# Attention with a fused GEGLU feed-forward on one core: cutting the work that is interleaved between attention passes into smaller pieces, reordering it, and moving loads

## The chip, the cores and the metric

The kernel runs on one core of a Trainium2 chip. The metric is the device time of one execution in microseconds (us). Times of engines, waits and transfers come from one profiled execution of each kernel.

## The reference

A pre-LayerNorm transformer layer in bf16: 2048 tokens, width 576, 32 heads of 18, feed-forward width 4608.

```python
def _A_ref(x, wqkv, wo):                      # attention, H = 32, Dh = 18
    ...
    scores = jnp.einsum("bhqd,bhkd->bhqk", q, k) * (Dh ** -0.5)
    p = _softmax(scores, axis=-1)
    o = jnp.einsum("bhqk,bhkd->bhqd", p, v)
    return (...)(o, 0, 2, 1, 3).reshape(B, S, D) @ wo

def _B_ref(x, w_gate, w_up, w_down):          # GEGLU, tanh gelu
    return (_gelu(x @ w_gate) * (x @ w_up)) @ w_down

h  = x + _A_ref(_layernorm(x), A_wqkv, A_wo)
h2 = h + _B_ref(_layernorm(h), B_w_gate, B_w_up, B_w_down)
```

## The kernel before

The tokens are cut into four blocks of 512 queries, each block into eight units of four heads, each unit into 32 passes. A *pass* is two score matmuls, one exponential and half a group of probability-times-value (PV) matmuls. Score tiles live in `Sring`, which has two slots, so PE can be at most two passes ahead of ACT:

```python
def emit_ST(i):                    # PE: two score matmuls of pass i
    ...
    slot = i % 2
    ...
    pe_group(fns, reads=[("KTj", s_), ("QTj", s_)], writes=wkeys)

def emit_EXP(i):                   # ACT: one exponential of 128x1024
    E("act", lambda e: e.activation(PT[:, pts, :], Sring[:, slot * 1024:(slot + 1) * 1024], ACTF.Exp, scale=SCALE),
      reads=[("S", slot * 2), ("S", slot * 2 + 1)], writes=[("PT", pts)])
```

Between passes the emitter puts *fillers*: pieces of the feed-forward (FFN) of the block before. A filler has a ready time in passes and a cost; each pass brings 560 of credit, and a filler is emitted whole:

```python
def run_fillers(i, budget):
    while urgent and urgent[0][0] <= i:
        _, _, fn = urgent.pop(0)
        fn()
    credit[0] = min(credit[0] + budget, 3 * budget)
    while bulk and bulk[0][0] <= i and credit[0] > 0:
        ready, cost, fn, tag = bulk.pop(0)
        fn()
        credit[0] -= cost
```

The FFN of one block has two halves of 18 gate/up steps and five down tiles each:

```python
def ffn_gate_up(f, slot, tail=False):         # PE: 5 + 5 matmuls, two evacuations
    ...
def ffn_gelu_a(f, tail=False):                # x*x (POOL; in the tail ACT), product (DVE), add (DVE; in the tail POOL)
def ffn_gelu_b(f):                            # tanh (ACT)
def ffn_gelu_c(f):                            # product (DVE), times up (POOL), into gT
def ffn_down(hf, m, slot):                    # PE: 18 matmuls, one evacuation
    ...
at(s0, 2200.0, ... ffn_gate_up(f, slot, tail=tl))
at(s0 + 2, 0.0, ... ffn_gelu_a(f, tail=tl))
at(s0 + 6, 0.0, ... ffn_gelu_b(f))
at(s0 + 8, 0.0, ... ffn_gelu_c(f))
...
at(s0 - 3, 0.0, ... ffn_load_wd(wslot, hf, m, barrier=(b == 0)))
at(s0, GS * 220.0, ... ffn_down(hf, m, wslot))
```

At a block's end come the output projection (Wo), LayerNorm 2 and its transposes, for four tiles of 128 rows. All loads go through one in-order queue, issued by SP; `jit_loads(u + 1)` fetches K, Q and V of the next unit eight passes ahead, as four K and four Q transfers of 19 partitions each:

```python
for c in range(4):
    j, r0 = head_loc(4 * g + c)
    pairs.append((KTj[32 * c:32 * c + PS, s_, :], KTd[r0:r0 + PS, j, :]))
...
    pairs.append((QTjm[32 * c:32 * c + PS, s_, c, :], QTd[r0:r0 + PS, j, b * QB:(b + 1) * QB]))
```

After the last block its own FFN is left over with no attention to lie between: the *tail*.

## Time and profile before

| stretch of the kernel before | from to (us) | what sets the pace |
|---|---|---|
| prologue and attention of block 0 | 0 to 426 | not touched by the change |
| three blocks with FFN fillers | 426 to 1512 | PE and ACT by turns |
| tail: Wo, LayerNorm 2 and the last FFN | 1512 to 1764 | one chain through DVE, POOL and ACT |

The median was 1767.25 us of four runs. These are the page's busy times (engine, busy us, share, instructions), its granted PE clock in 40 slices (tenths of full speed) and two of its costliest groups (busy, mean ns of one, then the idle time just before them and what ended it):

```profile
PE 1402.6 (80%) x7386; PEld 512.7 (29%) x7528; DVE 739.6 (42%) x1572; ACT 1109.5 (63%) x1293; POOL 370.4 (21%) x364
PEclk9778999999899999998999999989999999588988
L578 ACT ACTIVATE PT<-Sring 128x1024 bf16<-128x1024 f32 x1024 | 960.8, 1048 | 351.1 <-PE Sring L296 346.3
L296 PE MATMUL Sring<-QTjm,KTj 128*128 128x512 bf16 x1933 | 591.0, 388 | 133.3 <-ACT PT L578 105.0 <-issue 14.3 <-DMA QTjm<-QTd 9.3
```

Read the last two rows together. ACT stood idle 346 us in front of exponentials until PE had scores; PE stood idle 105 us in front of scores until ACT had emptied a slot. Two engines that wait for each other are the sign of pieces that are too coarse for the buffer between them.

### The profile page before, as it was taken

How to read it: one execution, taken by the hardware profiler on the slowest of the kernel's cores; microseconds unless marked ns; L12 is line 12 of the kernel's file. 1: busy time of each engine (PE TensorE's matmuls, PEld its weight loads, DVE VectorE, ACT ScalarE, POOL GpSimd, SP SyncE). 2: the span in 40 equal slices, each digit the busy share in tenths (PEclk: the TensorE clock that was granted, in tenths of full speed). 3: DMA queues.
4: the chain of work that ended last, by engine and by line, in shares of the span. 5: the costliest groups of instructions: out<-in, count | busy, mean ns of one | idle time of the engine just before them, and what ended most of it. 6: DMA issues, size and time to landing. Idle time of an engine off the chain costs nothing.

```text
span 1763.7 us, 20592 instructions
## 1 busy us (share of the span) xinstructions
PE 1402.6 (80%) x7386; PEld 512.7 (29%) x7528; DVE 739.6 (42%) x1572; ACT 1109.5 (63%) x1293; POOL 370.4 (21%) x364
## 2 busy tenths in 40 slices
PE   1558998887788899887898998878988988475765
PEld 0223332112232333233332332333323333321322
DVE  7546651002355046314551363144622651454352
ACT  2123789998577678676785786767866866133230
POOL 1000000000044034200340243003421430044251
PEclk9778999999899999998999999989999999588988
DMA  3010000000123212211232122111231221122332
GB/s 101 14 39 7 10 10 17 11 17 11 37 68 80 60 42 66 64 45 31 63 88 61 35 63 63 46 47 50 63 76 43 62 64 34 41 63 71 87 81 47
DMA packets 193173, 87.22 MB, mean 49 GB/s; under 512 B 97968, under 2 KB 190064, under 8 KB 193072
## 3 DMA queue, kind: packets, MB, share of 16 engines
q1 hardware_dynamic: 193072, 85.91, 18.2%
q8 instruction: 59, 0.97, 0.2%
q14 instruction: 42, 0.34, 0.1%
HBM read 71.07 MB, written 2.36 MB: 42 GB/s over the span
## 4 chain that ended last, share of the span: by engine, by line
PE 42%; ACT 20%; issue 19%; POOL 9%; DVE 8%; DMA 1%; SPq 1%; POOLq 0%; ACTq 0%; DVEq 0%
PE G L296 24%; ACT PT L578 19%; PE Sring L296 13%; POOL arena L721 3%; PE Aacc L297 3%; POOL arena L703 2%; POOL arena L700 2%; PE G L309 1%; SPq L288 1%; DVE arena L701 1%; POOL lnt L395 1%; DMA arena<-in_B_w_up_dram 1%; DVE kmx L437 1%; DVE kmx L439 1%; ACT arena L710 1%
## 5 line engine op out<-in xcount | busy, mean ns | idle before, releaser
L578 ACT ACTIVATE PT<-Sring 128x1024 bf16<-128x1024 f32 x1024 | 960.8, 1048 | 351.1 <-PE Sring L296 346.3
L296 PE MATMUL Sring<-QTjm,KTj 128*128 128x512 bf16 x1933 | 591.0, 388 | 133.3 <-ACT PT L578 105.0
L296 PE MATMUL G<-hnT,arena 128*128 128x512 bf16 x1421 | 356.0, 399 | 55.9 <-ACT arena L317 45.9
L296 PE MATMUL G<-arena 128*128 128x512 bf16 (+4 forms) x1112 | 267.4, 397 | 53.9 <-issue 40.9
L296 PEld LDWEIGHTS Sring<-QTjm,KTj 128*128 128x128 bf16 x2048 | 136.2, 98 | 434.1 <-ACT PT L578 331.5
L721 POOL TENSOR_TENSOR arena<-arena 128x512 bf16<-128x512 bf16 x144 | 166.2, 1154 | 392.9 <-DVE arena L719 384.9
L296 PEld LDWEIGHTS G<-hnT,arena 128*128 128x128 bf16 x1440 | 140.5, 101 | 248.9 <-ACT arena L317 64.6
L297 PE MATMUL Aacc<-PT,Vpj 128*32 128x512 bf16 x2048 | 205.9, 392 | 0.7 <-ACT PT L578 0.7
L719 DVE SCALAR_TENSOR_TENSOR arena<-arena 128x512 bf16<-128x512 bf16 x144 | 99.7, 692 | 178.7 <-ACT arena L710 178.7
L296 PEld LDWEIGHTS G<-arena 128*128 128x128 bf16 (+3 forms) x1120 | 118.3, 113 | 190.7 <-issue 91.3
L710 ACT ACTIVATE arena<-arena 128x512 bf16<-128x512 bf16 x144 | 91.6, 636 | 121.6 <-POOL arena L703 94.8
L701 DVE SCALAR_TENSOR_TENSOR arena<-arena 128x512 bf16<-128x512 bf16 x144 | 118.8, 825 | 104.7 <-POOL arena L700 104.1
L700 POOL TENSOR_TENSOR arena<-arena 128x512 bf16<-128x512 bf16 x108 | 112.4, 1041 | 199.0 <-DVE arena L322 199.0
L297 PEld LDWEIGHTS Aacc<-PT,Vpj 128*32 128x32 bf16 x2048 | 52.6, 93 | 221.6 <-issue 217.9
L324 DVE TENSOR_SCALAR arena<-G 128x512 bf16<-128x512 f32 x144 | 98.2, 682 | 13.4 <-PE G L296 13.4
L395 POOL TENSOR_TENSOR lnt<-lnt,halfc 128x1 f32<-128x1 f32 x32 | 17.6, 550 | 402.7 <-DVE lnt L394 342.2
L554 POOL COPY Vpj<-Vd 128x1152 bf16<-128x1152 bf16 x32 | 36.7, 1148 | 309.5 <-PE Aacc L297 296.0
L322 DVE CAST arena<-G 128x512 bf16<-128x512 f32 x108 | 73.8, 684 | 37.4 <-PE G L296 37.3
L598 DVE CAST a_sb<-Aacc 128x512 bf16<-128x512 f32 x32 | 22.1, 691 | 150.4 <-PE Aacc L297 150.2
L735 DVE COPY arena<-G 128x512 f32<-128x512 f32 (+1 forms) x20 | 13.8, 690 | 137.5 <-PE G L296 137.5
L317 ACT ACTIVATE arena<-G 128x512 bf16<-128x512 f32 x36 | 20.9, 580 | 65.4 <-PE G L296 65.4
L703 POOL TENSOR_TENSOR arena<-arena 128x512 bf16<-128x512 bf16 x36 | 41.4, 1150 | 56.7 <-DVE arena L701 56.7
(79 smaller groups left out, 556.3 us busy)
## 6 DMA issues: line engine op xcount, KB each, us to landing
arena<-in_B_w_gate_dram SPq DMA_DIRECT2D x72, 256.0 KB, 2.7
arena<-in_B_w_up_dram SPq DMA_DIRECT2D x72, 256.0 KB, 3.2
arena<-in_B_w_down_dram SPq DMA_DIRECT2D x32, 576.0 KB, 5.0
KTj<-KTd SPq DMA_DIRECT2D x128, 76.0 KB
QTjm<-QTd SPq DMA_DIRECT2D x128, 19.0 KB
arena<-in_A_x_dram SPq DMA_DIRECT2D x4, 576.0 KB, 3.9
h_sb<-in_A_x_dram SPq DMA_DIRECT2D x4, 576.0 KB, 5.9
arena<-in_B_w_gate_dram SPq DMA_DIRECT2D x72, 32.0 KB, 2.7
```

Of the source, the lines that this page charges most:

```text
L296: return lambda e: e.matmul(dst, lhsT, rhs, start=start, stop=stop)
L297: return lambda e: e.matmul(dst, lhsT, rhs, start=start, stop=stop, tile_position=tile_position, skip_group_check=skip)
L322: E("dve", lambda e: e.tensor_copy(dst_ap, src_ap), reads=reads, writes=writes)
L324: E("dve", lambda e: e.tensor_scalar(dst_ap, src_ap, scale, None, ALU.mult), reads=reads, writes=writes)
L554: E("pool", lambda e: e.tensor_copy(dst, src), reads=[("Vd", kt) for kt in range(NKT)] + [("Vd", kt, 1) for kt in range(NKT)], writes=[("V ...
L578: E("act", lambda e: e.activation(PT[:, pts, :], Sring[:, slot * 1024:(slot + 1) * 1024], ACTF.Exp, scale=SCALE), reads=[("S", slot * 2), ...
L700: E("pool", lambda e: e.tensor_tensor(x2, xb, xb, ALU.mult), reads=[("xb", k)], writes=[("x2", k)])
L701: E("dve", lambda e: e.scalar_tensor_tensor(out=x2, in0=x2, scalar=GC1, in1=xb, op0=ALU.mult, op1=ALU.mult), reads=[("x2", k), ("xb", k)], ...
L703: E("pool" if tail else "dve", lambda e: e.tensor_tensor(x2, x2, xb, ALU.add), reads=[("x2", k), ("xb", k)], writes=[("x2", k)])
L710: E("act", lambda e: e.activation(th, uu, ACTF.Tanh, scale=GC0), reads=[("x2", k)], writes=[("th", k)])
L719: E("dve", lambda e: e.scalar_tensor_tensor(out=x2, in0=th, scalar=1.0, in1=xb, op0=ALU.add, op1=ALU.mult), reads=[("th", k), ("xb", k)], ...
L721: E("pool", lambda e: e.tensor_tensor(gT[:, fs, :], x2, ub, ALU.mult), reads=[("ub", k), ("x2", k)], writes=[("gT", fs)])
```

## The change

Its intent is to make the fillers small enough for the two score slots, and to keep their inputs ready. Gate and up become two fillers of five matmuls; a down becomes three of six; Wo becomes 10 + 15, with all four Wo before the four LayerNorm-2 transposes; the second half of a gelu is emitted after the first half of the next one; down weights are prefetched, two tiles at a half's start; the next unit's K/Q/V load goes 24 instead of 8 passes ahead; the K projection of a tile is queued as five items instead of one.

```diff
-    def ffn_gate_up(f, slot, tail=False):
+    def ffn_gate(f, slot, tail=False):
         ...
+    def ffn_up(f, slot):
         ...
+    DCH = 3
-    def ffn_down(hf, m, slot):
+    def ffn_down_part(hf, m, slot, part):
+        ...
+        lo, hi = part * per, min(GS, (part + 1) * per)
+        ...
+        pe_group(fns, reads=[("wd", slot)] + [("gT", fs) for fs in range(lo, hi)], writes=[bkey])
 ... schedule_ffn ...
+                if fs == 0:
+                    for m in range(min(2, NIT)):
+                        at(s0, 0.0, ... ffn_load_wd(ws, hf, m, barrier=(b == 0)))
-                at(s0, 2200.0, ... ffn_gate_up(f, slot, tail=tl))
-                at(s0 + 2, 0.0, ... ffn_gelu_a(f, tail=tl))
-                at(s0 + 6, 0.0, ... ffn_gelu_b(f))
-                at(s0 + 8, 0.0, ... ffn_gelu_c(f))
+                at(s0, 1100.0, ... ffn_gate(f, slot, tail=tl))
+                at(s0 + 1, 1100.0, ... ffn_up(f, slot))
+                at(s0 + 3, 0.0, ... ffn_gelu_a(f, tail=tl))
+                if fs > 0:
+                    at(s0 + 5, 0.0, ... ffn_gelu_b(f - 1))
+                    at(s0 + 7, 0.0, ... ffn_gelu_c(f - 1))
 ...
-                at(s0 - 3, 0.0, ... ffn_load_wd(wslot, hf, m, barrier=(b == 0)))
-                at(s0, GS * 220.0, ... ffn_down(hf, m, wslot))
+                for part in range(DCH):
+                    at(s0 + part, 1320.0, ... ffn_down_part(hf, m, ws, part))
+                at(s0 + DCH - 1, 0.0, ... ffn_down_evac(hf, m))
+                if m + 2 < NIT:
+                    at(s0 + DCH - 1, 0.0, ... ffn_load_wd(ws, hf, m2))
 ... schedule_block_end ...
-            add_bulk(base + 7 + 2 * qt, 1800.0, ... block_Wo_qt(b, qt))
-            add_bulk(base + 9 + 2 * qt, 0.0, ... block_LN2_stats(b, qt))
-            add_bulk(base + 14 + 2 * qt, 600.0, ... block_LN2_T(b, qt))
+            add_bulk(base + 7 + 2 * qt, 900.0, ... block_Wo_qt_a(b, qt))
+            add_bulk(base + 8 + 2 * qt, 1100.0, ... block_Wo_qt_b(b, qt))
+            add_bulk(base + 8 + 2 * qt, 0.0, ... block_LN2_stats(b, qt))
+        for qt in range(4):
+            add_bulk(base + 17 + qt, 600.0, ... block_LN2_T(b, qt))
 ... main loop ...
-            if p == NPASS_U - 8:
+            if p == NPASS_U - 24:
                 if u + 1 < NU:
                     jit_loads(u + 1)
```

## The prediction

> **What bounds the kernel now.** Times are microseconds (us). One *pass* is two 128x512 score matmuls on PE, one 128x1024 exponential on ACT, and half a group of four PV matmuls; the program has 1024 of them, 256 for each block of 512 queries. Between passes the emitter puts *fillers*: the FFN of the block before. I first cut the span into stages (busy time of each engine by window; columns: stretch, length, busy time of PE, PEld, DVE, ACT, POOL with instruction counts, granted PE clock, DMA share, GB/s):
>
> ```profile
> 0.00:445.00 445.00, 321.13 (x1736) 113.46 (x1769) 186.33 (x436) 287.86 (x336) 22.77 (x40) 0.93 0.07 23
> 445.00:1506.00 1061.00, 918.05 (x4954) 329.44 (x5051) 435.71 (x928) 758.62 (x849) 262.56 (x248) 0.97 0.21 56
> 1506.00:1764.00 258.00, 163.43 (x697) 69.83 (x708) 117.53 (x209) 63.03 (x108) 85.09 (x76) 0.80 0.27 67
> ```
>
> Prologue and block 0 take 445, three blocks with FFN fillers 1061 (354 each), and a tail without attention 258. In the middle stretch PE is busy 87% and ACT 72%: neither is full, so one is being made to wait for the other. The timeline of PE shows how. First one period of gate/up filler (start, duration, idle before it):
>
> ```profile
> 656.06 2.32 PE L296 MATMUL G<-hnT,arena 128*128 128x512 bf16 x10
> 658.22 0.59 PE L296 MATMUL Sring<-QTjm,KTj 128*128 128x512 bf16 x2
> 658.75 0.40 PE L297 MATMUL Aacc<-PT,Vpj 128*32 128x512 bf16 x4
> 659.08 0.61 PE L296 MATMUL Sring<-QTjm,KTj 128*128 128x512 bf16 x2
> 659.93 0.60 PE L296 MATMUL Sring<-QTjm,KTj 128*128 128x512 bf16 x2 [0.25 <-ACT PT L578]
> ...
> 661.29 2.32 PE L296 MATMUL G<-hnT,arena 128*128 128x512 bf16 x10
> ```
>
> Ten filler matmuls hold PE for 2.16 (656.06 to 658.22); ACT, with room for two score tiles only, runs dry. Then four passes follow in which PE waits for ACT. Period 5.23. The down filler is longer, and the first down of each half also waits (the record says "issue") for the last gelu:
>
> ```profile
> 572.10 5.73 PE L296 MATMUL G<-arena 128*128 128x512 bf16 x18 [3.41 <-issue]
> 583.49 4.05 PE L296 MATMUL G<-arena 128*128 128x512 bf16 x18
> 593.62 4.06 PE L296 MATMUL G<-arena 128*128 128x512 bf16 x18
> ```
>
> One period is 10.13 with seven passes in it. At a block's end PE stands before the LayerNorm-2 transposes, which come right after the next Wo:
>
> ```profile
> 457.56 0.85 PE L309 MATMUL G<-ident,hn 128*128 128x128 bf16 x5 [4.25 <-DVE hn L404]
> ```
>
> The tail is another regime. One gate/up step there, DVE, POOL and ACT:
>
> ```profile
> 1563.63 0.69 DVE L719 SCALAR_TENSOR_TENSOR arena<-arena 128x512 bf16<-128x512 bf16 x1 [1.93 <-ACT arena L710]
> ...
> 1564.40 1.15 POOL L721 TENSOR_TENSOR arena<-arena 128x512 bf16<-128x512 bf16 x1 [1.47 <-DVE arena L719]
> 1564.84 1.26 DVE L701 SCALAR_TENSOR_TENSOR arena<-arena 128x512 bf16<-128x512 bf16 x1
> ...
> 1566.18 1.15 POOL L703 TENSOR_TENSOR arena<-arena 128x512 bf16<-128x512 bf16 x1 [0.63 <-DVE arena L701]
> ...
> 1567.36 0.63 ACT L710 ACTIVATE arena<-arena 128x512 bf16<-128x512 bf16 x1 [2.62 <-POOL arena L703]
> ...
> 1568.02 0.69 DVE L719 SCALAR_TENSOR_TENSOR arena<-arena 128x512 bf16<-128x512 bf16 x1 [1.92 <-ACT arena L710]
> ```
>
> This is one serial chain: second product (DVE), times up (POOL), first product of the next step (DVE), add (POOL), tanh (ACT), period 4.39, no engine full.
>
> **What the Trainium skill says.** "TensorE: Matmul & The Clock Gate", Part 1 (the HAM clock gate): a 512-column matmul starts every 215.7 ns warm and 426.7 ns cold, and PE goes cold after an idle window of about 3.4 us. The trace agrees: 2.16 / 10 = 216 ns here, and after the 3.41 wait above the 18 matmuls took 5.73 instead of 4.06. The same page, Part 3 (packing small matmuls): 32-column matmuls in different column groups run concurrently. So do the four PV matmuls: 0.33 for four (658.75 to 659.08). "SBUF — State Buffer", "Who interferes with whom": a DVE instruction with two SBUF inputs and a POOL instruction that reads SBUF exclude each other, for the whole instruction. The trace agrees: the first product takes 0.68 alone, but 1.26 when it starts inside L721, and ends at 1566.10, 0.55 after L721 (1565.55).
>
> **The change, part by part.** No instruction is added or removed on PE but the order changes; I read the order as built.
>
> (a) Gate and up (five matmuls each) become two fillers, and the built order is, over long stretches: four score matmuls, four PV, five filler matmuls. PE's need for four passes and one step: per two passes 0.43 + 0.53 + 0.33 = 1.29 (start-to-start above), per five fillers 1.08; together 2.37, for four passes 4.74. ACT's need: four exponentials at 0.94 (3.77 for four in the timeline) plus a tanh of 0.65 = 4.4. ACT can lag at most two tiles; laying the two out by hand (a score pair to its exponential's start 0.64, exponential 1.02, release 0.06) I find every score matmul's tile free at least about 0.0 to 0.7 before it is wanted, so PE should run without waiting. I take 4.78: saved 0.45 x 36 steps x 3 blocks = 49.
>
> (b) Down splits into 6 + 6 + 6. PE needs 7 x 0.645 + 3.88 = 8.4 against 10.13; ACT needs 6.6. Saved 1.73 x 10 x 3 = 52.
>
> (c) A part of down waits for its own six gT tiles only, and two more parts lie between it and the last gelu. The wait of 3.41 to 4.13 at six first downs, and about 1.5 of cold clock after each, go. I count 4.5 x 6 = 27.
>
> (d) All four Wo go before the four LN2 transposes; the DVE chain of one tile is 4.4 long and is now hidden under Wo and passes. Per block 4.25 + 1.3 (a smaller wait of the same kind) + about 1 cold = 6.5; x 3 = 20.
>
> (e) The gelu's second half of step f-1 goes behind the first half of step f. In the overlapped blocks this only adds latency that nobody waits for. In the tail it takes the tanh off the chain, but the two DVE products and the two POOL products still exclude each other: 0.6 + 0.69 + 1.15 + 1.15 = 3.59. So 4.39 becomes about 3.6, not the 2.3 that POOL alone would need: 0.8 x 36 = 29.
>
> (f) Tail, the rest: Wo and LN2 31 (7.6 each) becomes DVE-bound, about 2.6 + 4 x 4.4 + 3 = 23: 8. Down parts that start before the last gelu (idle there 9.05 and 8.80): about 3 each, 6.
>
> (g) Loads. Down weights are prefetched two at a half's start, in the one in-order queue before the second gate/up chunk. In the first FFN the two are chained by waits for landings: I estimate 6 lost. The next unit's K/Q load goes 24 instead of 8 passes ahead; no wait on it stood on the path (0.66 at 864), so nothing is gained, but its issue takes 11 in front of gate/up chunks; the three waits of about 1.1 for a chunk (503, 864, 1229) may come to some 3 each as steps get shorter: 6 more. Splitting the K tile filler changes nothing: the four parts have the same ready number, all urgent items that are ready are emitted at once, and the built PE order is identical up to the first Wo. So the first 445 stay.
>
> Sum: 49 + 52 + 27 + 20 - 12 = 136 in the blocks, 29 + 8 + 6 = 43 in the tail, 179 together: 1767 - 179 = 1588. Check from above: a block's PE need is 256 x 0.645 + 540 FFN matmuls x 0.216 + some 12 for Wo and transposes = 294, and some 40 passes without filler go at ACT's 0.92 instead of 0.645, 11 more: 305, against 354 - 136/3 = 309. The two agree.
>
> **The rivals.** First: ACT takes PE's place as what ends last. For it: ACT is within 7% of PE in the gate/up stretch (4.4 against 4.74), and a tanh that waits for DVE blocks the exponentials behind it. Against: a tanh is now emitted a whole step after its input is. If true, the step falls to 5.0 only and half of (a) is lost: about 1615. Second: DVE or the shared port. DVE needs 3.2 a step and the locked instructions about 4.0 (0.69 x 2 + 0.42 + 1.04 + 1.15) of 4.74; if evacuations get late, PE waits for a G bank. With three banks an evacuation has about two fillers' time (4.7) of slack. If it happened, steps stay near 5.2: about 1640. Third: in the tail the port lock doesn't bind (the skill's rule, one case in the trace): then the step falls to about 2.5 and the time to 1550. Fourth: the prefetched weights crowd the queue and each half's start stalls: + 3 to 5 at each of eight halves, about 1620. That all gain vanishes would need the filler gaps to come back elsewhere; with PE at 87% and ACT at 72% I see nothing that would hold it.
>
> **Range and chances.** Predicted 1588. Rivals one, two and four pull up, three down, so the range is lopsided: 1562 to 1630. 2% is 35 us; losing four fifths of the sum is needed to stay within it. Faster 0.97, same 0.02, slower 0.01.
>
> **What would show it.** In the profile after: gate/up periods of 4.7 to 4.9 with PE busy over 95% there and no wait for ACT between passes; downs at 8.4 to 8.7 per three parts; no wait of 3 to 4 before the first down nor before an hn transpose; tail steps of 3.5 to 3.7 with the two DVE products stretched; the time up to the first Wo unchanged. Gate/up at 5.2 with PE waiting for DVE, or ACT at 95%, would prove (a) wrong; tail steps at 4.4 or 2.5 prove (e) wrong.

## The result, and the profile after

The changed kernel takes 1596.74 us (median of 8 runs, 1596.11 to 1598.73), beside 1767.69 for the kernel before (13 runs, 1764.82 to 1770.59). The ratio is 0.9035, 95% interval 0.9026 to 0.9043: faster. A ratio is the mean time of one kernel's runs over that of the other's of the same rounds, so not quite the ratio of the medians. The result is 9 us above the 1588 predicted, inside the range.

The same lines of the page as before, and the same three windows of busy time by engine (the middle one is now 947 long instead of 1061, the tail 205 instead of 258):

```profile
PE 1345.6 (84%) x7386; PEld 509.7 (32%) x7528; DVE 761.7 (48%) x1572; ACT 1114.2 (70%) x1293; POOL 397.7 (25%) x364
PEclk9778999999988999999999999999999999979898
L578 ACT ACTIVATE PT<-Sring 128x1024 bf16<-128x1024 f32 x1024 | 976.7, 1040 | 255.9 <-PE Sring L296 254.0
L296 PE MATMUL Sring<-QTjm,KTj 128*128 128x512 bf16 x1963 | 567.5, 385 | 75.5 <-ACT PT L578 58.2
```

```profile
0.00:445.00 445.00, 324.14 (x1781) 115.47 (x1815) 189.37 (x450) 291.49 (x340) 23.42 (x42) 0.93 0.07 23
445.00:1392.00 947.00, 873.52 (x4909) 332.10 (x5005) 441.41 (x913) 759.00 (x846) 262.91 (x247) 0.98 0.25 64
1392.00:1597.00 205.00, 147.90 (x697) 62.10 (x708) 130.94 (x209) 63.75 (x109) 111.41 (x76) 0.89 0.32 80
```

Both mutual waits shrank: 346 to 254 and 105 to 58. In the middle stretch PE was idle for 1061 - 918 = 143 before and for 947 - 874 = 74 now. ACT's work there did not change (758.62 and 759.00).

For the reading by parts I cut both timelines of PE at the first matmul of each stage. Sums over the three blocks, and in brackets the exponentials in the stage (a pass on the edge counts twice):

| stage, three blocks | before | after | difference |
|---|---|---|---|
| first Wo to first gate | 119.2 (75) | 85.2 (69) | -34.0 |
| gate/up, both halves, with the wait before the first down | 604.4 (431) | 544.8 (419) | -59.6 |
| down of half 0 | 158.3 (108) | 140.3 (111) | -18.0 |
| down of half 1, to the next block's Wo | 203.7 (146) | 200.7 (167) | -3.0 |
| **blocks** | **1085.4** | **970.9** | **-114.5** |
| tail: Wo and LayerNorm 2 | 31.5 | 22.1 | -9.4 |
| tail: gate/up, two halves | 166.7 | 106.7 | -60.0 |
| tail: downs and end | 53.9 | 69.7 | +15.8 |
| **tail** | **252.1** | **198.5** | **-53.6** |

The first Wo came at 427.24 instead of 426.22: +1.0. Together -114.5 - 53.6 + 1.0 = -167.1, the difference of the two profiled spans. The last stage of a block seems to gain nothing, but over the three blocks it now holds 21 passes more: a block has a fixed 256 passes, and those that shorter fillers no longer cover are run at the end without fillers, some 0.92 each.

The timeline of PE in the gate/up stage after:

```profile
504.65 1.25 PE L296 MATMUL G<-hnT,arena 128*128 128x512 bf16 x5
505.74 1.03 PE L296 MATMUL Sring<-QTjm,KTj 128*128 128x512 bf16 x4
506.70 0.40 PE L297 MATMUL Aacc<-PT,Vpj 128*32 128x512 bf16 x4
507.03 1.25 PE L296 MATMUL G<-hnT,arena 128*128 128x512 bf16 x5
508.12 1.03 PE L296 MATMUL Sring<-QTjm,KTj 128*128 128x512 bf16 x4
509.08 0.40 PE L297 MATMUL Aacc<-PT,Vpj 128*32 128x512 bf16 x4
```

From 504.65 to 507.03 is 2.38: half a step with two passes, PE without a gap. The whole step is 4.76 instead of 5.23. The downs, by contrast, still have a wait in each period (only their own lines and the waits are shown):

```profile
563.05 1.46 PE L296 MATMUL G<-arena 128*128 128x512 bf16 x6
...
566.95 0.61 PE L296 MATMUL Sring<-QTjm,KTj 128*128 128x512 bf16 x2 [1.14 <-ACT PT L578]
...
573.00 1.47 PE L296 MATMUL G<-arena 128*128 128x512 bf16 x6
...
576.02 0.60 PE L296 MATMUL Sring<-QTjm,KTj 128*128 128x512 bf16 x2 [0.35 <-ACT PT L578]
```

The first down (563.05) starts with no wait before it, where the kernel before stood 3.41. The larger waits of PE in the first block's end and first FFN:

```profile
443.09 0.57 PE L309 MATMUL G<-ident,hn 128*128 128x128 bf16 x5 [1.42 <-DVE h_sb L654]
447.25 0.57 PE L309 MATMUL G<-ident,hn 128*128 128x128 bf16 x5 [1.79 <-DVE hnT L322]
459.72 2.31 PE L296 MATMUL G<-hnT,arena 128*128 128x512 bf16 x5 [5.60 <-DMA arena<-in_B_w_up_dram]
490.66 1.91 PE L296 MATMUL G<-hnT,arena 128*128 128x512 bf16 x4 [9.62 <-DMA arena<-in_B_w_up_dram]
```

The transposes (L309) no longer stand 4.25, but the first FFN waits 15.2 for its weights, where the longest such wait before was 3.61. The second of these loads stood directly behind a K/Q load in the queue (the queue's timeline):

```profile
469.37 2.50 SPq L288 DMA_DIRECT2D KTj<-KTd  x4
471.91 8.76 SPq L288 DMA_DIRECT2D QTjm<-QTd  x4
480.71 1.96 SPq L288 DMA_DIRECT2D arena<-in_B_w_gate_dram  x2
```

And one step of the tail:

```profile
1460.45 1.60 POOL L746 TENSOR_TENSOR arena<-arena 128x512 bf16<-128x512 bf16 x1
...
1461.19 1.41 DVE L744 SCALAR_TENSOR_TENSOR arena<-arena 128x512 bf16<-128x512 bf16 x1
...
1462.02 1.59 POOL L728 TENSOR_TENSOR arena<-arena 128x512 bf16<-128x512 bf16 x1
...
1463.13 1.03 DVE L726 SCALAR_TENSOR_TENSOR arena<-arena 128x512 bf16<-128x512 bf16 x1
...
1463.58 1.60 POOL L746 TENSOR_TENSOR arena<-arena 128x512 bf16<-128x512 bf16 x1
```

The step is 1463.58 - 1460.45 = 3.13 (4.39 before). POOL runs without a gap, but its operations are 1.60 long instead of 1.15.

### The profile page after: what moved, and what is told of

Same layout as the page of the kernel before. It is cut to its first block, busy times and chain, and to the rows that moved or that the text cites. A ratio compares the mean times of both kernels' runs of the same rounds, so it can differ in the third digit from the quotient of the medians.

```text
span 1596.6 us, 20508 instructions
## 1 busy us (share of the span) xinstructions
PE 1345.6 (84%) x7386; PEld 509.7 (32%) x7528; DVE 761.7 (48%) x1572; ACT 1114.2 (70%) x1293; POOL 397.7 (25%) x364
## 4 chain that ended last, share of the span: by engine, by line
PE 41%; issue 16%; ACT 13%; POOL 10%; DVE 9%; SPq 7%; DMA 4%; POOLq 0%; ACTq 0%; DVEq 0%
PE G L296 22%; PE Sring L296 15%; ACT PT L578 12%; SPq L288 7%; POOL arena L746 5%; PE Aacc L297 4%; DMA arena<-in_B_w_up_dram 3%; POOL arena L725 3%; POOL arena L728 1%; PE G L309 1%; POOL lnt L395 1%; DVE kmx L437 1%; DVE kmx L439 1%; DVE h_sb L654 1%; DVE stats L388 1%
## 5 line engine op out<-in xcount | busy, mean ns | idle before, releaser
L578 ACT ACTIVATE PT<-Sring 128x1024 bf16<-128x1024 f32 x1024 | 976.7, 1040 | 255.9 <-PE Sring L296 254.0
L296 PE MATMUL Sring<-QTjm,KTj 128*128 128x512 bf16 x1963 | 567.5, 385 | 75.5 <-ACT PT L578 58.2
L296 PE MATMUL G<-hnT,arena 128*128 128x512 bf16 x1402 | 360.1, 389 | 51.5 <-DMA arena<-in_B_w_up_dram 33.6
L296 PEld LDWEIGHTS Sring<-QTjm,KTj 128*128 128x128 bf16 x2048 | 161.7, 98 | 342.0 <-ACT PT L578 175.5
L746 POOL TENSOR_TENSOR arena<-arena 128x512 bf16<-128x512 bf16 x144 | 180.0, 1250 | 282.0 <-DVE arena L744 282.0
L296 PEld LDWEIGHTS G<-hnT,arena 128*128 128x128 bf16 x1440 | 125.4, 99 | 234.3 <-issue 53.2
L296 PEld LDWEIGHTS G<-arena 128*128 128x128 bf16 (+3 forms) x1120 | 113.6, 112 | 156.8 <-issue 48.1
L744 DVE SCALAR_TENSOR_TENSOR arena<-arena 128x512 bf16<-128x512 bf16 x144 | 128.4, 891 | 65.8 <-ACT arena L735 60.6
L725 POOL TENSOR_TENSOR arena<-arena 128x512 bf16<-128x512 bf16 x108 | 112.5, 1041 | 109.6 <-DVE arena L322 98.3
L726 DVE SCALAR_TENSOR_TENSOR arena<-arena 128x512 bf16<-128x512 bf16 x144 | 109.2, 758 | 46.4 <-POOL arena L725 46.0
L297 PEld LDWEIGHTS Aacc<-PT,Vpj 128*32 128x32 bf16 x2048 | 52.5, 92 | 219.7 <-issue 213.3
L598 DVE CAST a_sb<-Aacc 128x512 bf16<-128x512 f32 x32 | 22.1, 689 | 178.2 <-PE Aacc L297 178.2
L728 POOL TENSOR_TENSOR arena<-arena 128x512 bf16<-128x512 bf16 x36 | 56.4, 1565 | 39.3 <-DVE arena L726 39.3
```

The lines of the kernel that those rows point to most:

```text
L296: return lambda e: e.matmul(dst, lhsT, rhs, start=start, stop=stop)
L297: return lambda e: e.matmul(dst, lhsT, rhs, start=start, stop=stop, tile_position=tile_position, skip_group_check=skip)
L725: E("pool", lambda e: e.tensor_tensor(x2, xb, xb, ALU.mult), reads=[("xb", k)], writes=[("x2", k)])
L726: E("dve", lambda e: e.scalar_tensor_tensor(out=x2, in0=x2, scalar=GC1, in1=xb, op0=ALU.mult, op1=ALU.mult), reads=[("x2", k), ("xb", k)], ...
L728: E("pool" if tail else "dve", lambda e: e.tensor_tensor(x2, x2, xb, ALU.add), reads=[("x2", k), ("xb", k)], writes=[("x2", k)])
L744: E("dve", lambda e: e.scalar_tensor_tensor(out=x2, in0=th, scalar=1.0, in1=xb, op0=ALU.add, op1=ALU.mult), reads=[("th", k), ("xb", k)], ...
```

## The experiments

All twelve kernels gave correct results; runs of the kernel before: medians 1766.6 to 1770.3. "Against the changed kernel" is the difference of the medians to 1596.7. My theory was the prediction's list of parts; the rivals are in the expectations. e1 to e5 and e12 undo one part each, e6 to e9 alter one term, e11 puts one part alone into the kernel before, e10 combines.

| run | edit | median | ratio to before (95%) | against the changed kernel |
|---|---|---|---|---|
| e1_gu_joined | gate and up as one filler | 1650.2 | 0.9327 (0.9312, 0.9342) | +53 |
| e2_down_joined | down as one filler of 18 | 1674.4 | 0.9471 (0.9451, 0.9490) | +78 |
| e3_gelu_old | tanh and product not deferred | 1637.9 | 0.9254 (0.9234, 0.9274) | +41 |
| e4_wo_old | block end as before | 1638.0 | 0.9260 (0.9245, 0.9275) | +41 |
| e5_jit8 | K/Q/V load 8 passes ahead | 1677.0 | 0.9479 (0.9464, 0.9494) | +80 |
| e12_wd_late | down weights not prefetched | 1652.2 | 0.9346 (0.9323, 0.9368) | +55 |
| e11_before_jit24 | kernel before, K/Q/V load 24 ahead | 1817.1 | 1.0287 (1.0261, 1.0313) | (+49 on before) |
| e6_first_early | first FFN's weights loaded earlier | 1580.1 | 0.8930 (0.8913, 0.8946) | -17 |
| e7_jit_split | K/Q/V load in three parts | 1592.4 | 0.9001 (0.8985, 0.9017) | -4 |
| e8_tail_mult_dve | tail: one POOL product to DVE | 1596.9 | 0.9028 (0.9013, 0.9042) | 0 |
| e9_down5 | downs in parts of 5, 5, 5, 3 | 1578.1 | 0.8928 (0.8904, 0.8952) | -19 |
| e10_best | combination | 1521.3 | 0.8608 (0.8585, 0.8631) | -75 |

The seventh part of the change, the K tile filler, was not run: with the old filler put back, the built program has the same instructions in the same order on every engine.

### e1_gu_joined: gate and up in one filler again

```diff
-                at(s0, 1100.0, ... ffn_gate(f, slot, tail=tl))
-                at(s0 + 1, 1100.0, ... ffn_up(f, slot))
+                at(s0, 2200.0, ... (ffn_gate(f, slot, tail=tl), ffn_up(f, slot)))
```

> The changed kernel, but gate and up emitted together again as one filler of ten matmuls; the gelu order, down parts, Wo and loads stay changed. Theory (filler length: ACT runs dry behind ten matmuls): the period of a gate/up step in the blocks goes from 4.76 back to about 5.2, 108 steps x 0.45 = 49 us more, less some 8 us of weight-chunk waits that longer steps hide: 1632 to 1646 us; the tail stays at 198. Rival (the gelu's new place is what smooths the step): time stays within 5 us of 1597 and the step at 4.8.

Measured 1650.2, +53, a little over the range expected. The waits for ACT are back between passes (timeline of PE, one period):

```profile
652.82 2.33 PE L296 MATMUL G<-hnT,arena 128*128 128x512 bf16 x10
...
656.70 0.60 PE L296 MATMUL Sring<-QTjm,KTj 128*128 128x512 bf16 x2 [0.36 <-ACT PT L578]
657.62 0.60 PE L296 MATMUL Sring<-QTjm,KTj 128*128 128x512 bf16 x2 [0.31 <-ACT PT L578]
```

The gate/up stages took 97.1 to 98.4 where the changed kernel takes 87.5 to 88.9; the first, which also waits for its loads, took 108.9 instead of 103.3. The two-slot buffer is the reason that a filler's length matters: ten matmuls hold PE for 2.16, longer than the two exponentials (2 x 0.94) it can have stored.

### e2_down_joined: a down in one piece again

```diff
-    DCH = 3
+    DCH = 1
-                    at(s0 + part, 1320.0, ...
+                    at(s0 + part, GS * 220.0, ...
```

> The changed kernel, but each down is one filler of eighteen matmuls again (its weight prefetch stays as changed). Theory: down periods in the blocks go from 9.2 back to 10.3 to 11 us (1.3 x 30 = 39) and the first down of a half waits 3 to 4 us for the last gelu and runs cold (6 x 3 = 18 net of the 1.1 that is left now), and the tail's first downs start later, 2 x 3: 1640 to 1660 us. Rival (seven passes of ACT work hide behind a long filler anyway): under 1610 us.

Measured 1674.4, +78: more than I had expected. The down stage of half 0 went back to 53.5 (46.9 in the changed kernel), and the gate/up stages to 93 to 95 (the first to 108.9), because the wait before the first down is back inside them (569.26: 5.80 long, and the 18 matmuls after it took 6.61 instead of 4.06, cold, that is at the lower clock that PE is granted after such a wait). Splitting the down gave (b) and (c) of the prediction; as measured below they are worth some 32 and 27, 59 together. Most of the other 19 can be read from the trace: the waits before the six first downs are longer than in the kernel before, 5.58 to 6.19 each and 34.9 in all instead of 22.6, and the tail takes 5 more. PE's waits for weights are not the reason: 34.6 here, 35.2 in the changed kernel. So the parts are not independent. The deferred gelu, which this run keeps, may be what makes those waits longer; that was not run.

### e3_gelu_old: tanh and second product of a step not deferred

```diff
-                if fs > 0:
-                    at(s0 + 5, 0.0, ... ffn_gelu_b(f - 1))
-                    at(s0 + 7, 0.0, ... ffn_gelu_c(f - 1))
-                if fs == GS - 1:
-                    ...
+                at(s0 + 7, 0.0, ... ffn_gelu_b(f))
+                at(s0 + 9, 0.0, ... ffn_gelu_c(f))
```

> The changed kernel, but tanh and both products of a step again right behind its own first half. Theory: it matters in the tail alone: steps there go from 3.12 back to 4.39 us, 36 x 1.27 = 46, less about 6 because the first downs no longer wait for two steps' gelu at the end: 1632 to 1645 us, block stages unchanged within 2 us each. Rival: in the blocks the tanh blocks the exponentials behind it (DVE is behind), so block stages grow by 5 us or more each as well: over 1650 us.

Measured 1637.9, +41, in the theory's range. The tail's two gate/up stages took 74.8 and 73.7 instead of 52.5 and 54.2. The three blocks together took 970.1, in the changed kernel 970.9 (one by one within 4.1 us; single stages differ by up to 6.7, more than the 2 expected, because passes moved between them). One tail step, by its add on POOL and the tanh after it:

```profile
1482.07 1.15 POOL L728 TENSOR_TENSOR arena<-arena 128x512 bf16<-128x512 bf16 x1 [0.63 <-DVE arena L726]
1483.25 0.63 ACT L735 ACTIVATE arena<-arena 128x512 bf16<-128x512 bf16 x1 [2.62 <-POOL arena L728]
...
1486.46 1.15 POOL L728 TENSOR_TENSOR arena<-arena 128x512 bf16<-128x512 bf16 x1 [0.63 <-DVE arena L726]
```

1486.46 - 1482.07 = 4.39: exactly the chain of the kernel before, with its waits. So within the changed kernel the deferral gives the whole gain of the tail's steps and nothing in the blocks.

### e4_wo_old: the block end as before

```diff
-            add_bulk(base + 7 + 2 * qt, 900.0, ... block_Wo_qt_a(b, qt))
-            add_bulk(base + 8 + 2 * qt, 1100.0, ... block_Wo_qt_b(b, qt))
 ...
+            add_bulk(base + 7 + 2 * qt, 1800.0, ... (block_Wo_qt_a(b, qt), block_Wo_qt_b(b, qt)))
+            add_bulk(base + 9 + 2 * qt, 0.0, ... block_LN2_stats(b, qt))
+            add_bulk(base + 14 + 2 * qt, 600.0, ... block_LN2_T(b, qt))
```

> The changed kernel, but Wo in one filler per tile and each LayerNorm-2 transpose right after the next Wo, as before. Theory: waits of 4.25, 1.3 and 3 us for the LN2 chain come back in the three blocks and 7.6 us per tile in the tail: first Wo to first gate 38 instead of 26 us in a block (of which 2 us are passes moved elsewhere), 31 instead of 22 in the tail: 9 x 3 + 9 = 36, 1628 to 1640 us. Rival: with FFN loads waiting for their chunk at that place the block's gain is hidden, so only the tail's 9 us come back: about 1606 us.

Measured 1638.0, +41, in the range. First Wo to first gate: 42.7, 39.0, 38.0 again, and 31.5 in the tail. The waits of 3 to 5 before the transposes are back, such as one of 4.67 for hn at 457.47.

### e5_jit8: the next unit's K/Q/V load 8 passes ahead again

```diff
-            if p == NPASS_U - 24:
+            if p == NPASS_U - 8:
```

> The changed kernel with the next unit's K/Q/V load emitted 8 passes ahead again instead of 24. Theory (its issue, 11 us on the one in-order queue, delays a gate/up chunk wherever it stands, so the place matters little): number and size of the chunk waits change by under 5 us in all, 1592 to 1602 us. Rival (the earlier load is a gain of its own: scores waited for K/Q): 1605 us or more and PE waits for K/Q landings in the records.

My prediction says of this part that nothing is gained. Measured 1677.0: undoing it costs 80. The rival was true, and by far more than it said. Two of the twelve large waits (timeline of PE), and the queue's own timeline before the first of them:

```profile
498.97 1.86 PE L296 MATMUL Sring<-QTjm,KTj 128*128 128x512 bf16 x4 [4.74 <-issue]
...
638.68 1.87 PE L296 MATMUL Sring<-QTjm,KTj 128*128 128x512 bf16 x4 [7.68 <-issue]
```

```profile
479.82 2.50 SPq L288 DMA_DIRECT2D KTj<-KTd  x4
482.37 8.80 SPq L288 DMA_DIRECT2D QTjm<-QTd  x4
```

Before the first scores of a unit PE stood 4.69 to 7.68, twelve times, 71.8 in all, and the four score matmuls after each took 1.67 to 1.87 instead of 1.03 (cold clock). On the other side, the waits for gate/up chunks, 33.6 in the changed kernel, fell to 8.6: the 80 is what is left after that. The record calls the wait "issue", which hides the cause; three shorter ones of the same place are named "DMA QTjm<-QTd" (1.47 to 1.79). The load took 498.97 - 479.82 = 19.2 from its first issue to the start of the scores that waited for it, of which the issuing alone took 11.3 (to 491.17).

Why did the same position not hurt in the kernel before? A place in the queue is not a time. There, in the blocks with fillers, the K/Q load's first issue came at the latest 17 passes into the running unit, 19.5 us or more ahead of the next unit's first exponential, and just arrived (one wait, of 0.66). In e5, before each of the twelve long waits, it came 20 to 23 passes into the unit, so that the 19 us were not left. What stood directly in front of it was then a gate/up chunk that had waited for its buffer; prefetched down weights stood there only before the three shorter waits. Shorter passes (4.76 instead of 5.23 for four) take about 1.8 us from the last 15 passes, an estimate from these figures; the rest is that the chunk in front comes some passes later. Why it does, no run separates.

### e11_before_jit24: the early K/Q/V load alone, in the kernel before

```diff
-            if p == NPASS_U - 8:
+            if p == NPASS_U - 24:
```

> The kernel before with only the next unit's load emitted 24 passes ahead instead of 8. In the changed kernel the early load is worth 80 us (1677 without it). Theory (interaction: it takes some 19 us from first issue to last landing, and at the old pace it just arrives; only the shorter passes make it late): within 10 us of 1768. Rival (the load was late before as well, its wait recorded under another name): 1740 us or less.

Neither happened: 1817.1, which is 2.9% slower than the kernel before. PE now waits for down weights, 56.7 in all (timelines of PE and of the queue, first FFN):

```profile
580.27 6.48 PE L296 MATMUL G<-arena 128*128 128x512 bf16 x18 [9.48 <-DMA arena<-in_B_w_down_dram]
```

```profile
558.97 2.49 SPq L288 DMA_DIRECT2D KTj<-KTd  x4
561.51 9.26 SPq L288 DMA_DIRECT2D QTjm<-QTd  x4
570.81 9.79 SPq L288 DMA_DIRECT2D arena<-in_B_w_down_dram  x2
```

The K/Q load was emitted early and holds the in-order queue for 11.8 (558.97 to 570.77); the down weights, asked for only shortly before their down, stand behind it. From this I formed a new theory, that the early K/Q load pays only together with the down prefetch. e12 tests it from the other side.

### e12_wd_late: no prefetch of down weights

```diff
-                if fs == 0:
-                    for m in range(min(2, NIT)):
-                        at(s0, 0.0, ... ffn_load_wd(ws, hf, m, barrier=(b == 0)))
 ...
+                at(s0 - 3, 0.0, ... ffn_load_wd(ws, hf, m, barrier=(b == 0)))
                 for part in range(DCH):
                     at(s0 + part, 1320.0, ... ffn_down_part(hf, m, ws, part))
 ...
-                if m + 2 < NIT:
-                    at(s0 + DCH - 1, 0.0, ... ffn_load_wd(ws, hf, m2))
```

> The changed kernel, but each tile of down weights is asked for shortly before its down, as in the kernel before; gate/up fillers, parts of down, Wo order and the K/Q load 24 passes ahead stay. Theory (the K/Q load of 11.7 us in the one in-order queue is harmless only because the first two tiles of down weights already stand ahead of it): waits of 4 to 10 us for down weights come back at two or three downs of a block, as in the kernel before with the early K/Q load (56.7 us of such waits there, for +50 us), so +30 to +60 us: 1625 to 1660. Rival (the prefetch is not needed for its own sake: the parts of down start in a staggered way, and a load that is only 4 us late is absorbed): within 10 us of the changed kernel, 1587 to 1607.

Measured 1652.2, +55: the theory's range, though the longest waits were longer than the 4 to 10 it named. The waits for down weights, 62.4 in all (1.6 in the changed kernel), in two views as above:

```profile
564.63 2.74 PE L296 MATMUL G<-arena 128*128 128x512 bf16 x6 [12.90 <-DMA arena<-in_B_w_down_dram]
```

```profile
543.80 2.50 SPq L288 DMA_DIRECT2D KTj<-KTd  x4
546.35 8.76 SPq L288 DMA_DIRECT2D QTjm<-QTd  x4
555.15 9.82 SPq L288 DMA_DIRECT2D arena<-in_B_w_down_dram  x2
```

The first down of half 0 stood 12.90, 14.05 and 13.22 in the three blocks; two downs of half 1 (in the last block one) stood 3.5 to 4.2 each. With both loads moved (the changed kernel) neither waits. So at the new pace it costs 80 to drop one of the two load edits (e5) and 55 to drop the other. The new pace with neither load moved was not run, so what the two are worth together is not measured.

### e6_first_early: the first FFN's weights asked for before Wo

```diff
 ... at the first block's end, ahead of Wo and LayerNorm 2 ...
-            at(0, 0.0, wgu_zero)
-        at(0, 0.0, ... ffn_load_chunk(sl, 0, barrier=(b == 0)))
+            wgu_zero()
+            ffn_load_chunk(cbase % 2, 0, barrier=False)
+            ffn_load_chunk((cbase + 1) % 2, 1)
```

> The changed kernel with the memset and the first two gate/up chunks of the first FFN emitted at the block's end, ahead of Wo and LN2, and the down weights behind them. Theory: the waits of 5.60 and 9.62 us in the first FFN come from its loads being issued late and chained by landings; both go, with about 2 of cold clock: first Wo to first gate 26 instead of 32.5, first gate stage 88 instead of 103: 1576 to 1583 us. Rival (the wait of 9.6 is the K/Q load's queue time): only about 6 us are gained, 1590 us.

(The edit also drops the barrier of the first down-weight loads; the memset waits in its place.) Measured 1580.1, -17, in the theory's range. The waits of 5.60 and 9.62 are gone; first Wo to first gate took 26.7 and the first gate/up stage 87.6, like the other blocks. Of the cause of the 9.62 the rival was right in part: e5 and e7 left this FFN's own loads where they were, moved the K/Q load alone, and had no such wait either. The chunk was late because the K/Q load stood in front of it; asking earlier for the FFN's first weights also lets that K/Q load go earlier (447.13 instead of 469.37).

### e7_jit_split: K/V at pass 4, one half of Q at 12, the other at 20

```diff
-            if p == NPASS_U - 24:
-                if u + 1 < NU:
-                    jit_loads(u + 1)
+            if u + 1 < NU:
+                if p == 4:
+                    jit_loads(u + 1, split=True)
+                if p in (12, 20):
+                    jit_loads_q(u + 1, (p - 12) // 8)
```

> The changed kernel with the next unit's load cut in three (K and V at pass 4, Q halves at passes 12 and 20), so that no single issue of 11 us stands between two gate/up chunks. Theory: the six waits of 2.2 to 2.7 us for a chunk and the cold clock behind some of them go: 1597 - 15 to 1597 - 20, so 1577 to 1582 us. Rival (the transfer engines, not the queue's issue order, are what is late): waits stay and the time is within 4 us of 1597.

(Only the main loop's edit is shown; the helpers that cut the load are left out.) Measured 1592.4, -4: half right. The waits of 2.2 to 2.7 for gate/up chunks in mid-stage vanished (gate/up stages of 86.9 and 85.2), but the K part, emitted at pass 4, now stands in front of the first chunk of every FFN: first Wo to first gate took 36.0 to 36.2 in each block, and the waits for that chunk were 9.43, 10.24 and 10.08. (The first gate/up stage took 87.0 instead of 103.3; that is among the gains.) What was gained in one place was paid in another.

### e8_tail_mult_dve: in the tail, the second product of the gelu on DVE instead of POOL

```diff
-        E("pool", lambda e: e.tensor_tensor(gT[:, fs, :], x2, ub, ALU.mult),
+        E("dve" if tail else "pool", lambda e: e.tensor_tensor(gT[:, fs, :], x2, ub, ALU.mult),
```

> The changed kernel with the second product of the gelu in the tail moved from POOL to DVE. It measures what bounds the tail step: it is 3.12 us, two POOL instructions of 1.60 each back to back, where an exclusive port for whole instructions would give 3.59. Theory (the port is held for some 0.45 us of a DVE product and 1.1 of a POOL instruction, and POOL is full): POOL has one instruction a step, DVE five of 0.4 to 0.7, step 2.5 to 2.8: 36 x 0.45 = 16 less, 1577 to 1587 us. Rival (whole-instruction exclusion, or the chain over ACT bounds): step stays at 3.0 or more, within 5 us of 1597.

Measured 1596.9: no change, so "POOL alone is what holds the tail" fell. One step (DVE and POOL):

```profile
1459.99 1.53 POOL L728 TENSOR_TENSOR arena<-arena 128x512 bf16<-128x512 bf16 x1 [1.56 <-DVE arena L726]
...
1460.54 1.26 DVE L746 TENSOR_TENSOR arena<-arena 128x512 bf16<-128x512 bf16 x1
...
1461.73 0.68 DVE L324 TENSOR_SCALAR arena<-G 128x512 bf16<-128x512 f32 x1
```

POOL is half idle and the step is still 3.10 (the same L728 comes again at 1463.08). Now DVE is full: 0.68 + 0.68 + 0.68 + 1.26 = 3.30 of recorded time in 3.10, with ends overlapping. The bound moved from one engine to the other at nearly the same level. The time is the one that the rival gave. Of its two reasons the exclusion may have a part (L746, which runs beside POOL's L728, takes 1.26); the chain over ACT is not what the records show, since DVE does not idle. e10 takes one of these off DVE and agrees.

### e9_down5: downs in parts of 5, 5, 5 and 3

```diff
-    DCH = 3
+    DCH = 4
-                    at(s0 + part, 1320.0, ...
+                    at(s0 + part, 220.0 * (min(GS, 5 * (part + 1)) - 5 * part), ...
```

> The changed kernel with each down in parts of 5, 5, 5 and 3 matmuls with costs to match, instead of 6, 6 and 6. The downs in the blocks last 9.2 us, not the 8.4 predicted. Theory: the parts of six come every 2.36 passes, and in each pass that gets none PE waits about 0.4 us for a score tile to come free (score start to release 1.72 us); smaller parts come every two passes, so the wait goes: downs 8.5 us, 30 x 0.7 = 21 less, 1574 to 1584 us. Rival (seven passes' ACT work and the 64-column downs set the 9.2): within 5 us of 1597.

Measured 1578.1, -19, in the theory's range: down stages of half 0 took 44.0 to 44.3 instead of 46.7 to 46.9 with as many passes (37), the last stage of a block 67 instead of 69.8 (the last block's 58.0 instead of 61.2). A down took 8.78 ((606.73 - 571.61) / 4, from the second down to the next stage) where the changed kernel has 9.24. In the profiled runs the three blocks are 17.5 shorter and the tail, which the theory left out, 3.

### e10_best: what the others pointed to, together

The edits of e6, e8 and e9; K, V and the first half of Q at pass 8, the second half of Q at pass 16; LayerNorm-2 transposes two passes later; and in the tail the up evacuation on ACT:

```diff
-        evac(ub, bank[:, 0:512], [bkey], [("ub", k)], "dve", scale=0.5)
+        evac(ub, bank[:, 0:512], [bkey], [("ub", k)], "act" if tail else "dve", scale=0.5)
-            add_bulk(base + 17 + qt, 600.0, ... block_LN2_T(b, qt))
+            add_bulk(base + 19 + qt, 600.0, ... block_LN2_T(b, qt))
```

> The changed kernel with what the runs so far point to: first FFN's loads early (17 us gained alone), K/V and half of Q at pass 8 and the other half at pass 16 (the three-part version removed the mid-stage chunk waits but delayed each FFN's first chunk, since it stood ahead of it in the queue; here it doesn't), downs of 5, 5, 5, 3, LN2 transposes two passes later, and in the tail the second product on DVE and the up copy on ACT (ACT 2.4, DVE 1.8 and POOL 1.15 us a step, with the port about 2.5). If the gains add: 17 + 12 + 18 + 8 + 20 = 75, so 1522; expected 1510 to 1550 us. If the tail step stays near 3.1 and the downs at 9.2, 1555 to 1565.

Measured 1521.3 (1518.23 to 1522.59), ratio 0.8608 to the kernel before: it beats both kernels. Stages of the first block: 27.7, 86.0, 44.2, 86.1, 65.0; tail: 21.2, 45.2, 26.0, 45.3, 34.8. A tail step is now 2.50, by two of its adds on POOL:

```profile
1384.14 1.53 POOL L741 TENSOR_TENSOR arena<-arena 128x512 bf16<-128x512 bf16 x1 [0.97 <-DVE arena L739]
...
1386.64 1.54 POOL L741 TENSOR_TENSOR arena<-arena 128x512 bf16<-128x512 bf16 x1 [0.96 <-DVE arena L739]
```

3.10 - 2.50 = 0.60 is one evacuation on DVE (0.68 long, some 0.6 from start to the next start), and this agrees with e8's reading. That the K/Q split helps at passes 8 and 16 where it did little at 4, 12 and 20 was not run by itself; the sum of e6, e9, the tail and this split was expected at 1522.

## Why the prediction was right

The total was right within 9 us, but that it came so close is partly luck: errors of its sum cancelled. Predicted were 136 in the blocks and 43 in the tail, measured 114.5 and 53.6: downs and loads came out worse, block end and tail better.

**(a) Gate/up: right.** Predicted 4.78 a step, measured 4.76, with PE never waiting in the step; first and second rival (ACT or DVE bound there) are refuted by the same lines.

**(b) Downs: right in mechanism, too large.** Predicted 8.4 for three parts, measured 9.24 ((609.94 - 573.00) / 4, from the second down to the first gate of half 1) in half 0 and 10.03 in half 1. The step that failed is "PE needs 7 x 0.645 + 3.88 = 8.4": that sum counts PE's need alone, with no wait for ACT. But 7.25 passes do not divide evenly among three parts: these come two or three passes apart, and before the third pass a score matmul waits for its slot (the 1.14 and 0.35 above). The figure for the kernel before was read from one period, and the shortest kind: taken like the 9.24 it is 10.37 ((624.97 - 583.49) / 4), in half 1 11.06. So the term of 52 becomes (1.13 + 1.02) x 5 x 3 = 32. e9, which spreads the same 18 matmuls over four parts, saved 17 more in the blocks.

**(c) The wait before the first down: right** in the blocks: 3.41 to 4.14 at six downs gave way to none of more than 1.14, for ACT. The term of 27 holds: 22.6 of waits went, and the first downs, 8.3 longer in all than the others before, are 4.1 longer now: 22.6 + 8.3 - 4.1 = 27. In the tail the wait was 9.05 and 8.80 and is now 6.69 in each half (for POOL's last gT): the first two parts now start before it, so the wait moved into the down stage. That is most of the reason why the tail's downs and end rose by 15.8 and its gate/up fell by 60.0; under (f) 6 had been counted for this, and 4.5 of waits went.

**(d) Block end: too small.** Predicted 20, measured 34.0. Of this, six fewer passes in the stage, about 6 x 0.92 = 5.5, only moved to the block's end; 28 is left. The waits before the transposes shrank as counted, from 8.7 to 8.9 a block to 3.2. I had counted with them one cold stretch per block, not the cold clock of all the short Wo and transpose groups: the granted clock in this stage was 0.82 to 0.87 before and is 0.92 to 1.00 now. That the clock is the whole of the rest is not shown. e4 undoes this part for +41, tail included.

**(e) Tail step: right in mechanism, too long.** Predicted 3.6, measured 3.13, worth (3.6 - 3.13) x 36 = 17 more. It also lies outside the 3.5 to 3.7 that I had named as the sign. The step that failed is "exclude each other, for the whole instruction": I added the recorded lengths of both DVE products and both POOL operations end to end. The records show that POOL's operation grows from 1.15 to 1.60 while a DVE product is pending, that is by 0.45, not by the product's 0.69, and two such operations back to back are 3.2. The third rival (2.5, no exclusion) fell too.

**(f) Tail's Wo and LayerNorm 2:** predicted -8, measured -9.4. Right.

**(g) Loads: wrong in both directions.** The first FFN was predicted to lose 6; its gate/up stage took 103.3 beside 87.5 and 87.7 in the other blocks, so it lost 16, and e6 got 17 back; the longest of its waits, 9.62, was for a chunk directly behind the K/Q load. The chunk waits predicted at 3 each are six of 2.2 to 2.7. And the sentence "nothing is gained" from the early K/Q load is refuted by e5: it is worth 80 at the new pace, with the prefetch in place. The view I had relied on, that no wait for it stood on the path before, says what a load costs at the old pace only. The fourth rival (prefetched weights crowd the queue and each half stalls) happened in the first FFN alone; e12 shows that without the prefetch it is worse, +55. The early K/Q load needs the prefetch (e11: by itself, in the kernel before, it costs 49).

Put together for the blocks: (a) 0.47 x 108 = 51, (b) 32, (c) 27, (d) 28, and for (g) 16 in the first FFN and 9 for the other chunk waits (12.1 now, 3.3 before) to be taken off: 113, of the 114.5 measured.

**Splitting the K tile filler:** predicted nothing; the built order is the same, and the time to the first Wo differs by 1.0.

Not to be concluded: that the parts' worths add up. Undoing them one at a time costs 53 + 78 + 41 + 41 + 80 + 55 = 348, twice the 171 gained. Undoing one of the two loads even brings stalls that the kernel before did not have: 62.4 of waits for down weights in e12, 1.5 in the kernel before. What stays open is what the two load edits are worth together at the new pace, and why the first downs of e2 wait longer than those of the kernel before.

## What to carry to other kernels

When two engines wait for each other across a small ring, cut the work in between until one piece is shorter than what the ring stores, and spread it evenly: here pieces of five matmuls (1.08) beat six, and six beat eighteen. A place in an in-order load queue is not a time: after a change of pace or of any load's place, look again at what stands in front of every load, and do not take "no wait now" as "not needed". The K/Q loads are the next suspect: while they run the core's DMA rate falls to 8 to 31 GB/s and the engines' mean busy share to under a tenth, with one slice above (transfer rates of the changed kernel from 469 to 490, 40 slices):

```profile
DMA  9999300010000000000000000068615921278459
GB/s 228 275 282 277 78 16 8 8 23 8 31 23 23 31 23 31 23 23 31 23 23 31 23 31 23 23 179 248 176 32 145 312 66 49 75 197 266 125 155 308
```

The Trainium skill, "DMA: Bandwidth & Descriptors", section "Why a DMA increments its semaphore by 16 and not by 1", says that a transfer uses the largest number of engines, up to 16, that divides the slowest dimension (other than 1) of both sides, and that 127 partitions get one. 19 partitions would get one too. The trace agrees as far as it goes: from 472 to 482 of the changed kernel the mean busy share of the 16 engines was 0.06, one sixteenth, at 23 GB/s; but no run here changed the number of partitions, so this is not shown to be the cause.

## What the Trainium skill lacked or had wrong

- "SBUF — State Buffer", section "SBUF: two separate sides": of a DVE instruction with two SBUF inputs and a POOL instruction that reads SBUF, it says that whichever starts first gets the shared ports for the whole instruction. Recorded lengths can't be added on that ground: POOL's operation was stretched from 1.15 to 1.60, and a DVE product of 0.68 to 1.03 or 1.41, both ending 0.55 after POOL's operation did (tail of the changed kernel); step 3.13, not 3.59. Whether the ports are held for less than the instruction, or the record shows more than the time that they are held, no run here tells.
- "DMA: Bandwidth & Descriptors", "Issuing engines are not separate DMA queues": it says that the time to initiate a DMA is usually small beside the transfer. For the K/Q load here the issuing of eight transfers held the queue for 11.3 of the 19.2 from first issue to use (e5), and PE waited up to 9.48 (e11) and 14.05 (e12) for down weights that stood behind it.
- No page that I read says that a wait which goes away with an earlier load can be named "issue" by the profile's reader: twelve waits of 4.7 to 7.7 in e5 are so named.
